# Handing attention's output to the expert layer: chunks opened early, late parts split from SBUF

## The chip, the cores and the metric

One core of a Trainium2 chip runs the kernel. The metric is device time in microseconds, the median of three runs. Engines: TensorE (PE in the profile; PEld is its weight load), VectorE (DVE), ScalarE (ACT), GpSimd (POOL) and SyncE (SP), which issues all of this kernel's DMAs.

## The reference

```python
# attention: B, H, S, D = 4, 8, 576, 64
scores = where(causal, -1e9, q @ k.T / sqrt(D));  local = softmax(scores) @ v
q_p = where(q > 0, q, exp(q) - 1) + 1
mem_out = (q_p @ M_prev) / (q_p @ z_prev + 1e-6)
attn = g * mem_out + (1 - g) * local              # g = sigmoid(beta), one per head
# expert layer: x is attn as 2304 tokens x 512, d_ff = 2048
h = x @ w_in;  y = (h * sigmoid(1.702 * h)) @ w_out
```

## The kernel before

Attention works on 16 pairs of heads, p = 0 to 15: batch b = p // 4 and part c = p % 4 of the 512 model columns. Each pair's output, transposed, is `xf`, 128 columns of x by 576 tokens in SBUF (one buffer). The expert layer works on eight chunks of tokens: chunk 0 is the first 256 tokens of batch 0 and is made by a short separate prologue (`first_queries`); chunk 1 is the other 320 tokens of batch 0; chunks 2 and 3, 4 and 5, 6 and 7 are the halves (288 tokens) of batches 1, 2 and 3. A chunk needs all four parts c of its batch.

Expert input must be more exact than one pass of TensorE's 32-bit rounded format, so each x is split into a high part `xh` (a ScalarE copy with rounding) and the rest `xl` (a GpSimd subtraction). Both tiles have two buffers, so chunk n takes the buffers of chunk n - 2. A block is 128 of the 2048 hidden columns: 12 matmuls, for each part c `xh` times both halves of the weight and `xl` times the high one, gathered in one of two PSUM banks `pm`. `gate` (line 698) copies the result to `hk`, on VectorE and ScalarE in turn (line 703), and stores it to the DRAM tensor `gd`. After attention, w_out is converted and the second matmul (`acc`) runs over all tokens.

The program is written out in slots. `at(slot, prio, fn)` (line 81) books a step of attention in a slot; `step` (line 735) runs the steps of one slot and then lets the generator `first_moe` (line 708) emit expert matmuls as filler until an estimate of TensorE time is used up: PACE (line 41) gives 2.2 us per slot up to slot 59 and 2.7 from 60 on, and `mm` (line 86) counts columns / 2.4 + 13 ns for each matmul of attention and filler. A pair takes eight slots (seven in batch 0). What is emitted is then reordered on each engine when the program is built, with the order of emission as priority; at run time each engine, SP too, takes its queue in order.

How x comes to the expert layer: `xstore` (line 654), two slots after a pair's last matmuls (slots 13, 20, 27, 34 for batch 0, then 43, 51, 59, 67 and so on to 131), stores `xf` to the DRAM tensor `xd[b]` (line 655), and after the fourth pair notes `xready[b]`. When the generator comes to a chunk that is not planned, it yields until its batch is ready, and calls `plan_x` (line 688): one load of all four parts in the next slot (line 692), `split_x` (line 207) in the slot after it, first matmul in the third. Together with chunks 2, 4 and 6 the next chunk is planned too, one slot later.

Of the kernel before, what the change touches and what calls it, by code (L numbers as in the profile page):

```python
# [9 lines left out]
F32R = mybir.dt.float32r  # L10
# [5 lines left out]
B, H, S, D = 4, 8, 576, 64  # L16
NP = H // 2
# [4 lines left out]
NK = DM // 128  # L22
# [7 lines left out]
def f32(ap):  # L30
    return ap.bitcast(F32)
# [3 lines left out]
def tile_attention_memory_moe(ctx, tc, kq, vq, mem, zz, beta, w_in, w_out, out):  # L35
    nc = tc.nc
    CH = 288
    NCH = S // CH
    MB = 1
# [7 lines left out]
    def pool(stack, name, bufs=1, **kw):  # L47
        return stack.enter_context(tc.tile_pool(name=name, bufs=bufs, **kw))
# [4 lines left out]
    mop = pool(left, "mop", 2, side="left")  # L53
# [14 lines left out]
    xd = [dr.tile([128, NK, S], F32, name=f"xd{b}") for b in range(B)]  # L68
# [4 lines left out]
    state = {"slot": -8, "pe": 0.0, "seq": 0, "sum": 0, "bank": 0}  # L73
# [7 lines left out]
    def at(slot, prio, fn):  # L81
        assert slot > state["slot"], (slot, state["slot"])
        state["seq"] += 1
        events.setdefault(slot, []).append((prio, state["seq"], fn))

    def mm(out, l, r, start, stop):
        n = out.free_size()
        state["pe"] += (n / 2.4 + 13) / 1000
        if l.dtype == F32:
            state["pe"] += 3 * n / 2400  # L90
        nc.tensor.matmul(out, l, r, start=start, stop=stop)  # L91
# [5 lines left out]
    def copy(eng, dst, src, scale=None):  # L97
        if eng == "A":
            kw = {} if scale is None else {"scale": scale}
            nc.scalar.activation(out=dst, in_=src, func=AF.Copy, **kw)  # L100
        elif eng == "V":
            if scale is None:
                nc.vector.tensor_copy(dst, src)
            else:
                nc.vector.tensor_scalar(out=dst, in0=src, scalar1=scale, scalar2=None, op0=ALU.mult)
        else:
            nc.gpsimd.tensor_copy(dst, src)

    def tt(eng, dst, a, b, op):
        (nc.vector if eng == "V" else nc.gpsimd).tensor_tensor(out=dst, in0=a, in1=b, op=op)  # L110

    def sub(eng, dst, src, hi):
        tt(eng, dst, src, f32(hi), ALU.subtract)
# [82 lines left out]
    chunks = [(b, 0, 256) for b in range(MB)] + [(b, 256, 320) for b in range(MB)]  # L196
    chunks += [(b, CH * ch, CH) for b in range(MB, B) for ch in range(NCH)]
    XW = max(n for _, _, n in chunks)
    xq = {}
    xplan = {}  # L200

    def new_x(n):
        xl = mop.tile([128, NK, XW], F32R, name="xl")
        xq[n] = [None, xl]
        return xl

    def split_x(n):
        w, xl = chunks[n][2], xq[n][1]
        xh = xq[n][0] = mop.tile([128, NK, XW], F32R, name="xh")
        for c in range(NK):  # L210
            copy("A", xh[:, c, :w], f32(xl[:, c, :w]))
            sub("P", xl[:, c, :w], f32(xl[:, c, :w]), xh[:, c, :w])

    def first_queries(b):
        K, fsm = [], []
# [119 lines left out]
    pairs = [(b, c) for b in range(B) for c in range(NP)]  # L335
    raws = {}
    prep = {}
    xready = {}

    K0 = [STEP * p for p in range(MB * NP)]  # L340
    K0 += [(K0[-1] + 8 if K0 else 0) + 8 * p for p in range(len(pairs) - len(K0))]
# [168 lines left out]
    def plan_attend(p):  # L510
        b, c = pairs[p]
        k0 = K0[p]
        P = prep[p]
        U = {}
        rest = b < MB
        qo = 256 if rest else 0
# [135 lines left out]
            tt("V", P["xf"][r, q0:q0 + n], po[r, :n], xb[r, :n], ALU.add)  # L652

        def xstore():
            nc.sync.dma_start(xd[b][:, c, qo:], P["xf"][:, qo:])
            del prep[p]
            raws.pop(p)
            if c == NP - 1:
                xready[b] = state["slot"]

        at(k0, 10, s_tail)
        at(k0 + 1, 10, max_tail)
# [15 lines left out]
        for u, (h, j) in enumerate(order):  # L678
# [4 lines left out]
            if j < 0 or j == 3:  # L683
                at(k + 1, 32, lambda h=h, ch=int(j > 0): xsum(h, ch))
        at(k + 2, 60, xstore)


    def plan_x(n, slot):
        b, a, w = chunks[n]

        def load():
            nc.sync.dma_start(f32(new_x(n)[:, :, :w]), xd[b][:, :, a:a + w])

        at(slot + 1, 5, load)
        at(slot + 2, 45, lambda: split_x(n))
        return slot + 3

    def gate(ps, n, blk):
        b, a0, w = chunks[n]
        t0 = b * S + a0  # L700
        def keep():
            h = mop.tile([128, XW], F32, name="hk", bufs=3)
            copy("AV"[blk % 2 == 0], h[:, :w], ps[:, :w])
            nc.sync.dma_start(gd[blk][:, t0:t0 + w], h[:, :w])

        at(state["slot"] + 1, 28, keep)

    def first_moe():
        after = 0
        for n, (b, _, w) in enumerate(chunks):  # L710
            if n not in xplan:
                while b not in xready:
                    yield 1
                xplan[n] = plan_x(n, state["slot"])
                if n >= 2 * MB:
                    xplan[n + 1] = plan_x(n + 1, state["slot"] + 1)
            for blk in range(NB):
                while blk not in wb or n not in xplan or state["slot"] < xplan[n]:
                    yield 1
                after += len(moe_ps) > 1  # L720
                pp, nm = moe_ps[int(after > LATE)]
                ps = pp.tile([128, 512], F32, name=nm)
                wi = wb[blk]
                k = 0
                for c in range(NK):
                    for s, mv in ((0, 0), (1, 0), (0, 1)):
                        mm(ps[:, :w], wi[:, s, 128 * c:128 * c + 128], xq[n][mv][:, c, :w], k == 0, k == 3 * NK - 1)
                        k += 1
                    yield 0
                gate(ps, n, blk)  # L730
                yield 0
# [42 lines left out]
    for blk in range(W0, NB):  # L774
        at(CONV[blk - W0], 58, lambda blk=blk: conv_in(blk))
    fill["gen"] = first_moe()
    while state["slot"] < K0[-1] + 16:
        step()
# [134 lines left out]
```

## Time and profile before

| | us |
|---|---|
| median of three runs | 684.53 |
| lowest, highest | 683.67, 687.51 |
| the profiled execution | 687.52 |
| its span | 685.6 |

The page of the profile gives each engine's busy share of the span. The chain of work is the profile's walk back from the last instruction: at each step to what released it, or to the instruction before it on its engine. Tables by window give each engine's busy time in a stretch, the granted clock of TensorE as a share of full speed, and the DMA engines' busy share.

### The profile page before, as it was taken

Reading aid. Unit: us, or ns where it says so; the run is one execution under the profiler, and the core shown is the slowest. Engines: PE = TensorE matmul, PEld = TensorE weight load, DVE = VectorE, ACT = ScalarE, POOL = GpSimd, SP = SyncE. Lnnn points to the kernel's source line nnn. Section 1 sums busy time; section 2 is a strip of 40 time slices with the busy share of each in tenths; the row PEclk is TensorE's granted clock in tenths of the full one; section 3 lists DMA queues with packets and bytes.
Section 4 is the critical chain, followed back from the end, with each engine's and each line's share of the span. In section 5 each row is a group of like instructions: output and inputs, shape, how many; then the busy total and the mean of one; then the engine's idle time right before and its main releaser. Section 6 shows DMA issues by size and latency. Waiting matters only on the chain.

```text
span 685.6 us, 12438 instructions
## 1 busy us (share of the span) xinstructions
PE 629.7 (92%) x3984; PEld 572.3 (83%) x3984; DVE 435.1 (63%) x1112; ACT 396.4 (58%) x960; POOL 263.7 (38%) x303
## 2 busy tenths in 40 slices
PE   4578898799987799999899997999999999999997
PEld 3468686689986699999899997999888888888897
DVE  4987765776758776677657634816865555555453
ACT  5676546787757775777576533614555445454453
POOL 3647545976636793566475202502400000000000
PEclk8699999999999999999999999999999999999999
DMA  8859758888557765766772128936444335344231
GB/s 252 270 158 262 217 139 239 231 211 222 150 156 206 206 186 168 216 164 181 236 206 71 44 79 292 323 115 222 152 123 142 109 102 154 94 126 133 68 125 55
DMA packets 71425, 116.70 MB, mean 170 GB/s; under 512 B 8768, under 2 KB 41024, under 8 KB 71360
## 3 DMA queue, kind: packets, MB, share of 16 engines
q1 hardware_dynamic: 71360, 115.91, 57.8%
q8 instruction: 32, 0.52, 0.3%
q14 instruction: 33, 0.27, 0.1%
HBM read 63.97 MB, written 27.79 MB: 134 GB/s over the span
## 4 chain that ended last, share of the span: by engine, by line
PE 73%; DMA 10%; DVE 7%; ACT 5%; issue 3%; SPq 1%; POOL 1%; ACTq 0%; DVEq 0%; POOLq 0%
PE acc L91 29%; PE pm L91 24%; PE po L91 9%; PE pt L95 6%; PE ps L91 5%; DMA gd<-hk 2%; DMA qr<-in_vq_dram 2%; DMA xl<-xd 2%; DMA xd<-xf 1%; DVE ps L499 1%; DMA fq<-in_vq_dram 1%; DVE ws L180 1%; DVE wr L182 1%; DVE ws L179 1%; DMA mr<-in_mem_dram 1%
## 5 line engine op out<-in xcount | busy, mean ns | idle before, releaser
L91 PE MATMUL pm<-xh,wi 128*128 128x288 f32 (+2 forms) x1024 | 221.3, 305 | 12.3 <-ACT hk L100 6.0
L91 PEld LDWEIGHTS pm<-xh,wi 128*128 128x128 f32 x1024 | 168.0, 192 | 15.9 <-ACT hk L100 6.9
L91 PE MATMUL acc<-gh,wo 128*128 128x512 f32 (+1 forms) x640 | 179.2, 368 | 0.0
L91 PE MATMUL pm<-xl,wi 128*128 128x288 f32 (+2 forms) x512 | 153.6, 301 | 0.1
L91 PEld LDWEIGHTS acc<-gh,wo 128*128 128x128 f32 x640 | 115.1, 189 | 20.1
L91 PE MATMUL acc<-gl,wo 128*128 128x512 f32 (+1 forms) x320 | 115.1, 368 | 0.0
L91 PEld LDWEIGHTS pm<-xl,wi 128*128 128x128 f32 x512 | 98.1, 192 | 0.7 <-POOL xl L110 0.3
L508 POOL TENSOR_SCALAR a<-a,sm,g 128x512 f32<-128x512 f32 (+3 forms) x112 | 71.9, 654 | 64.3 <-DVE sm L547 37.1
L499 DVE CUSTOM_DVE_ANT_0 ps<-ps,mask 128x256 f32<-128x256 f32 (+4 forms) x144 | 69.3, 495 | 20.7 <-PE ps L91 15.5
L813 DVE SCALAR_TENSOR_TENSOR gt<-gt,graw 128x512 f32<-128x512 f32 (+1 forms) x80 | 52.3, 654 | 45.5 <-ACT gt L812 45.0
L91 PE MATMUL po<-e,vs 128*128 128x320 f32 (+3 forms) x416 | 76.3, 308 | 4.5 <-ACT e L100 3.7
L505 ACT ACTIVATE a<-ps,nm 128x512 f32<-128x512 f32 (+3 forms) x112 | 60.2, 540 | 31.9 <-DVE nm L499 26.8
L812 ACT ACTIVATE gt<-graw 128x512 f32<-128x512 f32 (+1 forms) x80 | 47.0, 589 | 54.6 <-DVE gl L110 54.6
L110 DVE TENSOR_TENSOR gl<-gt,gh 128x512 fp32r<-128x512 f32 (+1 forms) x80 | 53.2, 665 | 37.2 <-ACT gh L100 34.1
L110 DVE TENSOR_TENSOR e<-pt,e 128x320 fp32r<-128x320 f32 (+1 forms) x120 | 56.4, 486 | 30.9 <-ACT e L100 30.3
L100 ACT ACTIVATE e<-pt 128x320 fp32r<-128x320 f32 (+4 forms) x136 | 55.7, 435 | 28.0 <-PE pt L95 15.0
L91 PEld LDWEIGHTS po<-e,vs 128*128 128x128 f32 x416 | 64.1, 192 | 9.2 <-ACT e L100 4.3
L100 ACT ACTIVATE gh<-gt 128x512 fp32r<-128x512 f32 (+1 forms) x80 | 47.0, 588 | 42.2 <-PE acc L91 39.6
L91 PEld LDWEIGHTS acc<-gl,wo 128*128 128x128 f32 x320 | 59.4, 189 | 9.9
L91 PE MATMUL ps<-W 128*128 128x512 f32 (+3 forms) x224 | 58.6, 347 | 4.6 <-DVE e L110 2.8
L95 PE MATMUL pt<-ident,a 128*128 128x128 f32 x296 | 57.5, 276 | 0.4 <-ACT a L505 0.4
L100 ACT ACTIVATE hk<-pm 128x288 f32<-128x288 f32 (+2 forms) x64 | 26.2, 409 | 52.5 <-PE pm L91 40.4
(132 smaller groups left out, 962.9 us busy)
## 6 DMA issues: line engine op xcount, KB each, us to landing
graw<-gd SPq DMA_DIRECT2D x64, 256.0 KB, 2.7
gd<-hk SPq DMA_DIRECT2D x96, 144.0 KB, 2.5
wraw<-in_w_in_dram SPq DMA_DIRECT2D x16, 512.0 KB, 4.3
wraw<-in_w_out_dram SPq DMA_DIRECT2D x16, 512.0 KB, 4.6
kqr<-in_kq_dram SPq DMA_DIRECT2D x12, 608.0 KB, 5.3
W<-hi SPq DMA_DIRECT2D x24, 272.0 KB, 3.6
W<-loq SPq DMA_DIRECT2D x48, 128.0 KB, 3.7
W<-lok SPq DMA_DIRECT2D x32, 144.0 KB, 3.3
```

Source lines behind the costliest of these rows:

```text
L91: nc.tensor.matmul(out, l, r, start=start, stop=stop)
L95: nc.tensor.transpose(out, in_, idn)
L100: nc.scalar.activation(out=dst, in_=src, func=AF.Copy, **kw)
L110: (nc.vector if eng == "V" else nc.gpsimd).tensor_tensor(out=dst, in0=a, in1=b, op=op)
L179: nc.vector.tensor_scalar(out=si, in0=si, scalar1=3, scalar2=None, op0=ALU.logical_shift_left)
L180: nc.vector.scalar_tensor_tensor(out=si, in0=raw[:, :, 1], scalar=-2 ** 31, in1=si, op0=ALU.bitwise_and, op1=ALU.bitwise_or)
L182: nc.vector.scalar_tensor_tensor(out=box["r"].bitcast(I32), in0=raw[:, :, 0], scalar=29, in1=si, op0=ALU.logical_shift_right, op1=ALU.bitw ...
L499: nc.vector.tensor_tensor_reduce(out=ps, in0=ps, in1=mk, op0=ALU.add, op1=ALU.min, scale=-0.125, scalar=1e38 if j == 0 else nm[:, j - 1:j] ...
L505: nc.scalar.activation(out=a, in_=ps, func=AF.Exp, scale=-1.0, bias=nm, accum_out=sm)
L508: (nc.vector if eng == "V" else nc.gpsimd).tensor_scalar(out=a, in0=a, scalar1=r, scalar2=gcol, op0=ALU.mult, op1=ALU.mult)
L812: nc.scalar.activation(out=t[:, :n], in_=raw[:, :n], func=AF.Tanh, scale=0.851)
L813: nc.vector.scalar_tensor_tensor(out=t[:, :n], in0=t[:, :n], scalar=1.0, in1=raw[:, :n], op0=ALU.add, op1=ALU.mult)
```

## The change

`plan_x` and `xready` go. A chunk is opened (`open_x`) when the generator comes to it, whether or not its batch is complete; with chunks 2, 4 and 6 the next one is opened too. Opening takes the buffers of `xl` and `xh`; each part that was stored by then is loaded by a DMA of its own, in the same slot, and split two slots later. A pair whose chunks are open when its `xstore` comes is no longer stored: `xf` is split straight into the chunks' `xh` and `xl`, and the first matmul may be emitted in the next slot after the fourth part.

```diff
-    def split_x(n):
-        w, xl = chunks[n][2], xq[n][1]
-        xh = xq[n][0] = mop.tile([128, NK, XW], F32R, name="xh")
-        for c in range(NK):
-            copy("A", xh[:, c, :w], f32(xl[:, c, :w]))
-            sub("P", xl[:, c, :w], f32(xl[:, c, :w]), xh[:, c, :w])
+    stored = {b: [] for b in range(B)}
+    left_x = {}
+
+    def split_x(n, c, src):
+        w = chunks[n][2]
+        xh, xl = xq[n]
+        copy("A", xh[:, c, :w], src)
+        sub("P", xl[:, c, :w], src, xh[:, c, :w])
+        left_x[n].discard(c)
+        if not left_x[n]:
+            xplan[n] = state["slot"] + 1
+
+    def open_x(n):
+        b, a, w = chunks[n]
+        xl = new_x(n)
+        xq[n][0] = mop.tile([128, NK, XW], F32R, name="xh")
+        left_x[n] = set(range(NP))
+        for c in stored[b]:
+            nc.sync.dma_start(f32(xl[:, c, :w]), xd[b][:, c, a:a + w])
+            at(state["slot"] + 2, 45, lambda c=c: split_x(n, c, f32(xl[:, c, :w])))
...
         def xstore():
-            nc.sync.dma_start(xd[b][:, c, qo:], P["xf"][:, qo:])
+            mine = [n for n, ch in enumerate(chunks) if ch[0] == b and (ch[1] or not rest)]
+            if any(n in left_x for n in mine):
+                for n in mine:
+                    split_x(n, c, P["xf"][:, chunks[n][1]:chunks[n][1] + chunks[n][2]])
+            else:
+                stored[b].append(c)
+                nc.sync.dma_start(xd[b][:, c, qo:], P["xf"][:, qo:])
             del prep[p]
             raws.pop(p)
-            if c == NP - 1:
-                xready[b] = state["slot"]
...
-    def plan_x(n, slot):
-        b, a, w = chunks[n]
-
-        def load():
-            nc.sync.dma_start(f32(new_x(n)[:, :, :w]), xd[b][:, :, a:a + w])
-
-        at(slot + 1, 5, load)
-        at(slot + 2, 45, lambda: split_x(n))
-        return slot + 3
...
-            if n not in xplan:
-                while b not in xready:
-                    yield 1
-                xplan[n] = plan_x(n, state["slot"])
+            if n >= MB and n not in left_x:
+                open_x(n)
                 if n >= 2 * MB:
-                    xplan[n + 1] = plan_x(n + 1, state["slot"] + 1)
+                    open_x(n + 1)
```

## Rows read from the trace of the kernel before

**Rows 1.** The page, part 1: busy us (share) x instructions of each engine.

```profile
PE 629.7 (92%) x3984; PEld 572.3 (83%) x3984; DVE 435.1 (63%) x1112; ACT 396.4 (58%) x960; POOL 263.7 (38%) x303
```

**Rows 2.** The chain of work over the span: start us, us, what.

```profile
...
228.93 4.46 DMA xd<-xf
233.40 4.48 DMA xl<-xd
...
416.05 7.23 DMA xl<-xd
...
435.25 49.32 PE pm L91 x372
484.57 197.13 PE acc L91 x960
```

**Rows 3.** Table by window: stretch, length, busy us (instructions), granted clock, DMA share, GB/s.

```profile
131.00:145.00 14.00, 9.62 (x55) 8.09 (x55) 8.04 (x33) 10.28 (x29) 11.03 (x13) 0.88 0.92 253
145.00:188.00 43.00, 43.00 (x320) 42.44 (x318) 32.85 (x104) 31.87 (x88) 29.04 (x33) 1.00 0.69 188
...
210.80:228.90 18.10, 13.62 (x93) 11.19 (x92) 15.29 (x51) 14.30 (x42) 11.69 (x14) 1.00 0.75 201
229.60:238.40 8.80, 6.08 (x46) 5.31 (x44) 6.46 (x18) 4.83 (x15) 4.24 (x5) 1.00 0.74 212
...
336.00:346.00 10.00, 7.77 (x50) 7.52 (x49) 5.99 (x24) 6.37 (x19) 7.70 (x10) 0.83 0.56 166
...
420.00:435.00 15.00, 11.08 (x69) 10.38 (x67) 12.31 (x19) 9.96 (x21) 7.29 (x7) 0.89 0.96 334
```

**Rows 4.** Timelines of ScalarE, VectorE and TensorE: start us, us [idle before, releaser].

```profile
130.61 0.43 ACT L100 ACTIVATE xf<-po 64x320 f32<-64x320 f32 x1 [0.37 <-PE po L91]
145.07 0.83 PE L91 MATMUL pm<-xh,wi 128*128 128x320 f32 x4
204.08 0.31 PE L91 MATMUL pm<-xl,wi 128*128 128x320 f32 x1
233.48 0.48 DVE L110 TENSOR_TENSOR xf<-po,xb 64x320 f32<-64x320 f32 x1 [2.10 <-DMA xd<-xf]
238.40 0.79 PE L91 MATMUL pm<-xh,wi 128*128 128x288 f32 x4 [1.27 <-ACT xh L100]
```

**Rows 5.** Timeline of SP's queue: start us, us of the issue, line, transfer.

```profile
132.87 0.38 SPq L655 DMA_DIRECT2D xd<-xf  x1
...
332.40 1.47 SPq L692 DMA_DIRECT2D xl<-xd  x1
...
343.00 0.57 SPq L692 DMA_DIRECT2D xl<-xd  x1
...
353.48 0.54 SPq L655 DMA_DIRECT2D xd<-xf  x1
```

**Rows 6.** Groups by shape: count, busy us, mean ns, idle before.

```profile
L110 POOL TENSOR_TENSOR xl<-xl,xh 128x288 fp32r<-128x288 f32 x24 | 18.6, 809 | 36.3 <-ACT xh L100 36.3
...
L100 ACT ACTIVATE xh<-xl 128x288 fp32r<-128x288 f32 x24 | 8.7, 435 | 5.9 <-DMA xl<-xd 5.8
```

**Rows 7.** Waits (us, times, longest): 334 to 346, 420 to 436; SP's, whole span.

```profile
PE pm L91 <- ACT hk L100: 2.2, 1, 2.2
...
ACT xh L100 <- DMA xl<-xd: 3.0, 1, 3.0
...
ACT ws L172 <- DMA wraw<-in_w_out_dram: 2.2, 1, 2.2
...
SPq L692 <- PE pm L91: 3.7, 2, 2.4
```

**Rows 8.** DMA issues over the span: transfer, count, KB each, median us to landing.

```profile
gd<-hk SPq DMA_DIRECT2D x96, 144.0 KB, 2.5
...
W<-loq SPq DMA_DIRECT2D x48, 128.0 KB, 3.7
...
xl<-xd SPq DMA_DIRECT2D x6, 576.0 KB, 5.2
```

More of the change, by code (lines that the diff above doesn't have):

```diff
@@ L337, in tile_attention_memory_moe @@
     prep = {}
-    xready = {}
     K0 = [STEP * p for p in range(MB * NP)]
```

## The prediction

> **What bounds the kernel now.** I read the page's first part, the chain, the windows, then the queues at the places the chain names. The page says TensorE is busy 92% of a 685.6 us span [rows 1]. That figure flatters: matmuls overlap, so I take free TensorE time from the weight loads (83% busy) as window length less PEld busy. Where the granted clock of a window is below 1.00, part of it ran at 1.2 GHz instead of 2.4, and I add the length times the missing share.
>
> The chain's order of time [rows 2] shows what sets the end: from 435.25 us on, nothing but TensorE (49.32 us of expert input, then 197.13 us of expert output). Ahead of that, the chain runs through x: the store of pair 7 at 228.93 takes 4.46 us, the load behind it 4.48 us, and at 416.05 a load takes 7.23 us. From 145 to 188, PEld is busy 42.44 of 43 us [rows 3]: TensorE is the bound there, as it is at the end. So a microsecond of expert work moved into a free place earlier is a microsecond off the end, as long as attention does not itself become the bound.
>
> Free places: the first matmul of chunk 1 starts at 145.07, its last at 204.08, the first of chunk 2 not before its split allows, at 238.40 [rows 4]. Ahead of each, attention runs alone with much of TensorE free (6.9 us in 210.8 to 228.9 [rows 3]). Two smaller holes lie at 336 to 346 and 420 to 435.
>
> The slots in the code are only priorities: chunk 5's load, emitted in slot 110, stands at 343.00, ahead of pair 12's store of slot 107, at 353.48 [rows 5]. Each engine's queue is reordered when the program is built; what counts is when data and buffers are there.
>
> **Which parts go direct.** By the code's own costs, eight slots of attention take 11.05 us, so PACE leaves 6.55 us of filler per eight slots up to slot 59 and 10.55 later. Chunk 1 is 16 blocks of 12 x (320/2.4 + 13) ns = 28.1 us. Before: pair 3 stores in slot 34, first block in slot 37, last in 67. After: chunk 1 is opened in slot 13 (reached there already), part 0 is loaded (its store has just been issued), parts 1 to 3 come direct, and the first block may follow in slot 35. Three periods give 19.7 us, the last 8.4 us some six slots: chunk 2 is reached in slot 65, two ahead of pair 7's xstore in slot 67. So chunks 2 and 3 load parts 0 to 2 and take part 3 direct. Their 51 us last some 39 slots from 68: chunk 4 is reached in slot 107, after pair 11 (99); chunk 6 in 139, after pair 15 (131). These get no direct part, only four small loads in place of a large one.
>
> **The change part by part.**
>
> (a) Chunk 1. Now: pair 3's store at 132.87, the load behind it, first matmul at 145.07 [rows 4, 5]. After: xf is complete at 131.04 [rows 4], well before SP came to its store; one ScalarE copy of 0.43 us and one GpSimd subtraction of 0.81 us [rows 6] make part 3 ready at 132.3, or by 134 where GpSimd's queue holds it. The free time in 131 to 145 is 14 - 8.09 = 5.9 us, plus 0.12 x 14 = 1.7 us of clock [rows 3]. Upper bound: 7.6, and with two blocks' parts 0 to 2 (there are two pm banks; 18 x 0.146 = 2.6 us) begun earlier, some 8 of what can follow through. Lower bound: 0, if batch 1's attention does not move up when TensorE is relieved. I take 5, nearer the top, as 145 to 188 has no free TensorE time.
>
> (b) Chunk 2. The same step at 228.93: first matmul at 230 to 231 in place of 238.40 [rows 2, 4]. Free there: 8.8 - 5.31 = 3.5 us [rows 3]. The first two blocks' parts 0 to 2 can go into the 6.9 us free before it: 18 x 0.133 = 2.4 us. Bounds 2 and 6; I take 4.5.
>
> (c) Chunk 4. ScalarE stands still for 3.0 us on the load that went out at 332.40; the hk copy is queued behind, both pm banks fill, TensorE idles 2.2 us [rows 5, 7] and comes back at 1.2 GHz for a part (granted 0.83 over this window [rows 3]). In all 2.5 + 1.7 = 4.2 us. After: parts 0 to 2 were stored long ago and can be loaded as soon as chunk 2's buffer is free; only a quarter of the bytes follows the last store. Bounds 0 and 4.2; I take 2.5.
>
> (d) Chunk 6. The same at 416.05, but here ScalarE also waits 2.2 us for w_out [rows 7], with the DMA engines 96% busy [rows 3]. Hole: 4.6 + 1.65 = 6.3 us. The w_out waits stay. Bounds -1 (more requests in a full queue) and 6; I take 2.
>
> (e) DMA. Gone: four stores (3 x 160 KB, 288 KB) and as many bytes of load, 1.5 MB; at the 253 GB/s of 131 to 145, 6 us of transfer where DMA is 92% busy [rows 3]. Issues on SP: 16 stores and 7 loads become 12 and 23, so 12 more at 0.38 to 0.57 us [rows 5], 5 to 7 us of SP in bursts of six and eight at chunks 2, 4 and 6. Behind them stand attention's W copies and the gd stores. I set both at nothing together: the bursts are hidden where parts were stored long before; without that cover, each costs up to 8 x 0.57 - 2 x 0.57 = 3.4 us.
>
> A 576 KB load lands in 5.2 us, a 144 KB gd store in 2.5 and 128 KB W copies, four of them in a row, in 3.7 each [rows 8]: less than two in turn would take, so small requests overlap. The Trainium skill speaks against the split loads: "DMA: Bandwidth & Descriptors", section "Bandwidth", asks for batches of 1 MiB and more, and its section "Anatomy of one DMA" (the GpSimd path) fits a fixed 2 us per DMA beside bytes over 436 GB/s. By that, an estimate from the page, one 576 KB load takes 3.4 us (the row has 5.2) and a 144 KB one 2.3 (the row agrees with 2.5), so four in a row 9.4; six us more at chunks 4 and 6, with (c) and (d) lost, would make 671 + 12 + 4.5 = 687.5 us, near the slower rival below. As the rows overlap, I don't take it.
>
> (f) ScalarE and GpSimd. The splits stay 28 and 28, only earlier. At pair 7 two copies (0.87 us) and two subtractions (1.62 us) stand in front of the next pair's work; GpSimd is busy 11.69 of 18.1 us there [rows 3], so hidden, or 1.6 us once. xf has one buffer; its next writer waited 2.10 us for the store [rows 4], and now waits for the subtraction instead. Nothing, or a small gain; I count nothing.
>
> Sum: 5 + 4.5 + 2.5 + 2 = 14 us. The profiled execution took 687.52 us around its 685.6 us span, 3 us above the median; I take the difference to the median, 684.53 - 14 = 670.5, say **671**. All low ends give 1 us, all high ones 24; for this case alone 664 to 679.
>
> **The rivals.**
> 1. Attention's own chain sets batch 1's end, so (a) is lost: 4.5 + 2.5 + 2 = 9, **675.5 us**. For it: a pair alone took 18.1 us from store to store (210.80 to 228.93) with TensorE free by a third. Against: 145 to 188 is full.
> 2. Filler is only shifted: (a) nothing, (b) its low 2, (c) and (d) nothing, as the reordered queues put the last part's copy where the load stood: **682.5 us**, no difference.
> 3. Slower: the loads at chunks 4 and 6 arrive later than the one large load. SP issues eight, four of which hold for the matmuls of the chunk before (L692 waited on TensorE for 3.7 us in all, twice [rows 7]); they go through one after another at 2.5 us each, 10 in place of 5.2; ScalarE's queue stands on the last part, hk copies and TensorE behind it. Each place: 4.8 + 2.4 and 1 us of clock = 8.2, so 684.5 - 9.5 + 16.4 = **691 us**. It decides from about 6.5 us at each place. Against it: parts 0 to 2 need no recent store.
> 4. The change doesn't do what it says: chunk 2 is reached after pair 7 and loads all four parts, (b) is lost: 5 + 2.5 + 2, **675 us**. Two slots stand between.
>
> **How the numbers follow.** Forecast 0.62, rival 1 0.13, rival 2 0.13, rival 3 0.08, rival 4 0.04. A measurement of this kernel tells some 0.5% (3.4 us) from no change. Faster: 0.62 + 0.13 + 0.04 = 0.79; same 0.13; slower 0.08. The range 663 to 683 takes in the forecast's own and rivals 1, 2 and 4, less the outer tails.
>
> **What would show it.** (a) first matmul of chunk 1 at 131 to 135, and pair 7's part up to 5 us earlier. (b) no store for pair 7, and TensorE on chunk 2 within 3 us of xf. (c), (d) no 3 us wait of ScalarE on xl at chunk 4, and a shorter one at chunk 6. (e) 12 stores and 23 loads. I am wrong if the chunk starts move up and pair 7's end doesn't, or if SP's bursts hold up W copies.

## The result and the profile after

| | before | after |
|---|---|---|
| median of four runs, us | 684.10 | 692.34 |
| lowest, highest | 682.67, 687.51 | 690.91, 693.09 |
| the profiled execution (its span) | 687.52 (685.6) | 693.09 (691.3) |

After / before is 1.0111, with a 95% interval of 1.0069 to 1.0153: slower by some 8 us, where 13 us faster was forecast. Of both kernels the slowest of the four runs is the profiled one, so the spans differ by 5.7 us and the medians by 8.2.

The page of after, part 1, as [rows 1]: busy us (share) x instructions.

```profile
PE 633.6 (92%) x3984; PEld 575.3 (83%) x3984; DVE 432.3 (63%) x1112; ACT 397.8 (58%) x960; POOL 265.4 (38%) x303
```

No engine has noticeably more work than before. So the time was lost in waiting, and the chain says for what. After's chain over the span, as [rows 2]: start us, us, what.

```profile
172.14 5.46 DMA xl<-xd
...
198.59 5.96 DMA xl<-xd
...
288.88 5.13 DMA xl<-xd
...
340.80 4.83 DMA xl<-xd
...
419.99 2.95 DMA xd<-xf
...
439.90 26.98 PE pm L91 x191
...
469.70 20.81 PE pm L91 x156
490.51 197.14 PE acc L91 x960
```

The last stage is as long as before (197.14 and 197.13 us) and begins at 490.51 in place of 484.57; all of the loss lies ahead of it. The loads of x stand on the chain at four places spread over the span; in [rows 2] two were read, both behind the last store of a batch.

The change was built as the slot count of the prediction said. After's DMA issues, as [rows 8] (transfer, count, KB each, median us to landing), show 12 stores and 23 loads; of pairs 1, 2, 3 and 7 no store is left.

```profile
gd<-hk SPq DMA_DIRECT2D x96, 144.0 KB, 2.4
W<-loq SPq DMA_DIRECT2D x48, 128.0 KB, 3.5
xd<-xf SPq DMA_DIRECT2D x11, 288.0 KB, 2.8
xl<-xd SPq DMA_DIRECT2D x22, 144.0 KB, 4.5
...
xd<-xf SPq DMA_DIRECT2D x1, 160.0 KB, 3.1
xl<-xd SPq DMA_DIRECT2D x1, 160.0 KB, 2.8
```

A load of 144 KB lands after 4.5 us (median), a 576 KB load of before after 5.2 [rows 8]. A quarter of the bytes saves 0.7 us.

Waits over the whole span (total us, times, longest), before:

```profile
ACT xh L100 <- DMA xl<-xd: 6.0, 4, 3.0
```

And after:

```profile
ACT xh L100 <- DMA xl<-xd: 22.4, 10, 4.5
```

ScalarE stood 22.4 us on loads of x, ten times, where it stood 6.0 us, four times. SP's queue in after (start us, us of the issue, line, transfer) shows why there are so many:

```profile
165.72 0.41 SPq L676 DMA_DIRECT2D xd<-xf  x1
...
172.14 0.42 SPq L227 DMA_DIRECT2D xl<-xd  x1
...
281.98 0.54 SPq L676 DMA_DIRECT2D xd<-xf  x1
...
288.88 0.57 SPq L227 DMA_DIRECT2D xl<-xd  x1
...
289.98 0.42 SPq L227 DMA_DIRECT2D xl<-xd  x1
```

The store of pair 4 goes out at 165.72 and the load of that part for chunk 2 6.4 us behind it; behind pair 9's store at 281.98 come the first two loads for chunk 4, at 288.88 and 289.98, when chunk 2's buffers have just come free. By the prediction's count opening emitted these loads in slots 65 and 107, but once each part has its own load, each can be moved forward in the reordered queue until it stands behind its own store or the release of its buffer, and its xh copy with it. ScalarE's timeline in after (start us, us [idle before, releaser]):

```profile
136.57 1.22 ACT L100 ACTIVATE hi<-kqr 128x1216 fp32r<-128x1216 f32 x1 [2.15 <-DMA qr<-in_vq_dram]
137.70 0.45 ACT L100 ACTIVATE xh<-xf 128x320 fp32r<-128x320 f32 x1
...
177.62 0.44 ACT L100 ACTIVATE xh<-xl 128x288 fp32r<-128x288 f32 x1 [3.29 <-DMA xl<-xd]
177.97 0.85 ACT L100 ACTIVATE e<-pt 128x384 fp32r<-128x384 f32 x2
...
294.03 0.44 ACT L100 ACTIVATE xh<-xl 128x288 fp32r<-128x288 f32 x1 [3.80 <-DMA xl<-xd]
294.38 0.48 ACT L100 ACTIVATE e<-pt 128x384 fp32r<-128x384 f32 x1
```

Behind each waiting copy stands attention's own work, the softmax copy `e`, up to 3.29 and 3.80 us late. (Such waits alone don't show a loss: e1 below has 13.0 us of them and loses nothing.) Before, one load of all four parts could not go ahead of the batch's last store, so its split never stood in front of the attention that makes the batch.

Windows of after, as [rows 3], and some more (stretch, length, busy us of PE, PEld, DVE, ACT, POOL with instructions, granted clock, DMA share, GB/s):

```profile
131.00:145.00 14.00, 10.19 (x50) 8.45 (x48) 7.55 (x28) 9.52 (x25) 12.30 (x14) 0.76 0.82 212
145.00:188.00 43.00, 42.12 (x305) 41.12 (x306) 29.15 (x96) 27.85 (x77) 21.77 (x26) 1.00 0.58 165
...
420.00:435.00 15.00, 13.26 (x97) 12.55 (x96) 8.48 (x15) 6.69 (x14) 3.83 (x3) 1.00 0.84 298
```

```profile
197.00:217.00 20.00, 14.72 (x85) 12.69 (x83) 11.56 (x39) 11.71 (x33) 10.71 (x11) 0.83 0.59 164
285.00:320.00 35.00, 33.78 (x257) 32.71 (x255) 22.85 (x68) 20.27 (x57) 17.15 (x20) 1.00 0.73 200
320.00:335.00 15.00, 13.30 (x100) 13.02 (x101) 11.56 (x40) 13.03 (x37) 10.83 (x12) 1.00 0.51 137
335.00:352.00 17.00, 14.12 (x96) 13.56 (x95) 9.80 (x31) 9.61 (x29) 8.21 (x10) 0.90 0.69 201
445.00:484.00 39.00, 37.88 (x288) 37.64 (x287) 16.66 (x31) 10.24 (x23) 8.08 (x6) 1.00 0.56 183
```

The same five of before:

```profile
197.00:217.00 20.00, 17.12 (x114) 14.58 (x115) 15.88 (x54) 13.86 (x40) 13.41 (x14) 1.00 0.59 158
...
285.00:320.00 35.00, 35.00 (x275) 34.80 (x274) 26.47 (x88) 24.61 (x70) 18.55 (x22) 1.00 0.68 190
320.00:335.00 15.00, 15.00 (x116) 14.79 (x115) 10.07 (x31) 11.03 (x30) 8.59 (x10) 1.00 0.81 221
335.00:352.00 17.00, 14.77 (x102) 14.30 (x101) 10.12 (x34) 13.18 (x39) 13.50 (x16) 0.90 0.72 194
445.00:484.00 39.00, 39.00 (x298) 39.00 (x297) 18.25 (x34) 12.05 (x26) 6.81 (x6) 1.00 0.55 179
```

With free time as length less PEld, as in the prediction, the same view gives for the whole stretch from 97 to 484:

| us | 97–197 | 197–217 | 217–260 | 260–285 | 285–335 | 335–400 | 400–484 |
|---|---|---|---|---|---|---|---|
| before | 17.0 | 5.4 | 10.6 | 0.2 | 0.4 | 3.0 | 4.9 |
| after | 15.6 | 7.3 | 6.9 | 0.3 | 4.3 | 3.9 | 7.3 |

The holes that the change aimed at did become smaller (97 to 197 by 1.4 us, 217 to 260 by 3.7). But 1.9 us came back at 197 to 217, where chunk 1, begun earlier, was used up earlier and the clock now fell to 0.83 (part of the window at 1.2 GHz), 3.9 at 285 to 335, which had been full, and 3.3 from 335 on. The sum grows by 3.9 of the 5.9 us by which the last stage begins later. The table leaves out the clock, since work at the lower clock takes longer but counts as busy: 131 to 145 was granted 0.76 against 0.88 [rows 3], 197 to 217 0.83 against 1.00. By the prediction's own rule (length times the missing share), summed over windows of 8 us from 97 to 484, the clock took 10.2 us in after and 6.7 in before. Free time and clock together grow by 7.4 us, more than the 5.9.

### The profile page after: what moved, and what is told of

Read it like the earlier page. It is cut to its first block, busy times and chain, and to the rows that moved or that the text cites. A ratio compares the mean times of both kernels' runs of the same rounds, so it can differ in the third digit from the quotient of the medians.

```text
span 691.3 us, 12443 instructions
## 1 busy us (share of the span) xinstructions
PE 633.6 (92%) x3984; PEld 575.3 (83%) x3984; DVE 432.3 (63%) x1112; ACT 397.8 (58%) x960; POOL 265.4 (38%) x303
## 4 chain that ended last, share of the span: by engine, by line
PE 67%; DMA 13%; ACT 7%; DVE 5%; SPq 4%; issue 3%; POOL 1%; ACTq 0%; DVEq 0%; POOLq 0%
PE acc L91 29%; PE pm L91 21%; PE po L91 7%; PE ps L91 5%; PE pt L95 5%; DMA xl<-xd 3%; DMA kqr<-in_kq_dram 3%; DMA gd<-hk 2%; DMA xd<-xf 1%; ACT a L520 1%; DMA qr<-in_vq_dram 1%; SPq L419 1%; ACT e L100 1%; DMA wraw<-in_w_in_dram 1%; DMA vr<-in_vq_dram 1%
## 5 line engine op out<-in xcount | busy, mean ns | idle before, releaser
L110 DVE TENSOR_TENSOR gl<-gt,gh 128x512 fp32r<-128x512 f32 (+1 forms) x80 | 53.3, 666 | 37.2 <-ACT gh L100 34.0
L91 PE MATMUL ps<-W 128*128 128x512 f32 (+3 forms) x224 | 60.6, 356 | 5.3 <-DVE e L110 2.6
```

## The experiments

Each kernel was run in five rounds beside the kernel before; ratios are to that, with a 95% interval. The kernel before itself gave single times between 678.7 and 688.8 us, so only ratios are compared, and a mechanism seen in one trace counts as an indication where no ratio stands behind it. "The changed kernel" (ratio 1.0111) is the reference for the experiments that start from it.

### The change in parts: e1, e2, e3

The chunks in a set are opened as in the changed kernel; the others are planned as before (complete batch, one load).

```diff
-            if n >= MB and n not in left_x:
+            if n in NEW and n not in left_x:         # e1: (1,)  e2: (1, 2, 3)  e3: (4, 5, 6, 7)
                 open_x(n)
...
+            elif n >= MB and n not in NEW and n not in xplan:
+                while len(stored[b]) < NP:
+                    yield 1
+                open_old(n, state["slot"])
...
```

> Only chunk 1 is opened early (part 0 loaded, parts 1 to 3 direct); chunks 2 to 7 come by store and one load, as before. Theory W (ScalarE's in-order queue stands on loads of parts that were stored a moment before, so the early and split loads cost): there is one such load here, at 98, where TensorE waited 1.3 us, so nothing is lost and the 2.3 us of early matmuls at 97 to 131 are kept: 680 to 684 us against 684. Rival C (opening chunk 1 early is itself the loss, as pair 4's store was already 4.5 us late in the changed kernel): 687 to 690 us.

Measured: 684.93 beside 684.23, ratio 1.0012 (0.9985 to 1.0039). Chunk 1 alone is worth nothing. SP's queue in this kernel, the stores of pairs 4 and 7:

```profile
167.36 0.39 SPq L693 DMA_DIRECT2D xd<-xf  x1
...
231.85 0.54 SPq L693 DMA_DIRECT2D xd<-xf  x1
```

Pair 4 is stored at 167.36 (before 161.27) and pair 7 at 231.85 (before 228.93 [rows 2]): 6 and 3 us later. Of both, 2 us were there from pair 0 on (96.81 and 94.83), so attention lost 4 us up to the first pair of the batch and 1 us up to its last. It did not move up. Chunk 2 needs that last pair, so it could begin no earlier, while chunk 1 ended 7 us earlier (last matmul at 197.01, before 204.08 [rows 4]).

The early matmuls did fill free places: from 97 to 484 free TensorE time is 38.3 us, before 41.5. But the clock, by the rule above, took 11.8 us where it took 6.7. The stretch behind chunk 1 in e1, and ScalarE's waits on loads of x over its span:

```profile
197.00:217.00 20.00, 15.05 (x92) 13.81 (x91) 13.34 (x46) 13.52 (x39) 10.75 (x12) 0.83 0.53 148
```

```profile
ACT xh L100 <- DMA xl<-xd: 13.0, 6, 4.8
```

> Chunks 1 to 3 as in the changed kernel, chunks 4 to 7 as before. Theory W: the waits of ScalarE at 174 to 177 and around 200 to 206 stay (some 6 us of free TensorE time), the earlier start of chunk 2 (6 us) stays too, the waits at 290 to 408 go: 683 to 687 us. Rival C: 690 us or more, little better than the changed kernel's 692.

Measured: 691.95, ratio 1.0110 (1.0075 to 1.0144): the whole loss, with chunks 4 to 7 as before. The step from e1 to e2 is chunks 2 and 3: three small loads each and one direct part. Windows of e2:

```profile
285.00:335.00 50.00, 50.00 (x389) 49.51 (x388) 36.33 (x116) 35.28 (x98) 26.38 (x29) 1.00 0.71 194
335.00:352.00 17.00, 11.82 (x71) 11.59 (x71) 8.56 (x31) 11.44 (x33) 14.20 (x18) 0.80 0.58 177
```

TensorE is full from 285 to 335, where after lost most, and then waits 5.18 us for chunk 4's split, until 340.68. The whole loss thus comes without the hole at 285 to 335.

> Chunks 1 to 3 as before, chunks 4 to 7 opened as in the changed kernel: four loads of 144 KB each in place of one of 576 KB, nothing direct. Theory W: ScalarE waits some 3 to 4 us on each of three or four loads, TensorE loses 2 us at each: 688 to 692 us against 684. Rival C: 683 to 685 us, no loss.

Measured: 686.93, ratio 1.0040 (1.0010 to 1.0069). Nothing is direct here; four small loads in place of one cost 2.7 us. ScalarE's waits on loads of x are 15.5 us in six (6.0 in four before), and 285 to 335 is no longer full (PEld 45.40 of 50 us). The two parts do not add up: 1.0110 and 1.0040 alone, 1.0111 together.

### Whose queue the splits stand in: e4, e5

e4: the changed kernel, with the xh copies of direct parts on VectorE. e5: the changed kernel, with those of loaded parts on GpSimd, so that ScalarE waits for no load of x.

```diff
-        copy("A", xh[:, c, :w], src)
+        copy(eng, xh[:, c, :w], src)     # e4: "V" if src is xf, else "A";  e5: "P" if src is xl, else "A"
```

> The changed kernel, but the high parts of direct parts are copied by VectorE and not by ScalarE. Theory L (the gain at chunk 1 was lost because pair 3's copy stands in ScalarE's queue behind the hi copy, which waits for a load until 136.6): chunk 1 begins about 3 us earlier, 688 to 690 us against the changed kernel's 692. If ScalarE's place in the order doesn't matter there: 691 to 693.

Measured: 691.26, ratio 1.0105 (1.0070 to 1.0141), no better than the changed kernel. In ScalarE's queue the direct copy of pair 3 stood behind `hi` until 137.70 (above); it is free of that here, and 131 to 145 has more work in it (PEld 10.89 us at full clock, in after 8.45 at 0.76), but the total stays. So the late direct copy was not the cause.

> The changed kernel, but the high parts of loaded parts are copied by GpSimd (which does their subtraction anyway), so ScalarE's queue never stands on a load of x. Theory W (ScalarE's waits for the split loads are the loss): 685 to 689 us against the changed kernel's 692. Theory P (chunks 2 and 3's matmuls, emitted two slots earlier, take TensorE from attention and run out earlier at the next chunk): 691 to 693 us.

Measured: 687.99, ratio 1.0058 (1.0024 to 1.0091). ScalarE waits for no load of x here, and the point estimate lies 0.5% below the changed kernel's. The intervals overlap, so it is not shown that half of the loss hangs on these waits; and e1 (13.0 us of them, no loss) and e2 (12.6 us, the whole loss) say that their total does not set the time.

### One load, and a later place: e6, e7, e8

e6: one load for all parts that are stored when a chunk is opened. e7: the first matmul of chunks 2 and 3 may be emitted in the third slot after the last part instead of the first (slot 70, as before, instead of 68). e8: both.

```diff
-        for c in stored[b]:
-            nc.sync.dma_start(f32(xl[:, c, :w]), xd[b][:, c, a:a + w])
+        k = len(stored[b])
+        nc.sync.dma_start(f32(xl[:, :k, :w]), xd[b][:, :k, a:a + w])
...
-            xplan[n] = state["slot"] + 1
+            xplan[n] = state["slot"] + (3 if n in (2, 3) else 1)
```

> The changed kernel, but the parts that are stored when a chunk is opened come by one load each chunk (parts 0 to 2 for chunks 2 and 3, all four for chunks 4 to 7), so nothing is loaded and split behind each single pair. Theory W: three early waits at chunks 2 and 3 become one, those at 4 to 7 are as before the change: 685 to 688 us. Theory P: 690 to 693 us.

Measured: 690.24, ratio 1.0080 (1.0052 to 1.0108). Windows of e6:

```profile
285.00:320.00 35.00, 35.00 (x275) 34.80 (x275) 27.09 (x88) 24.75 (x69) 18.30 (x20) 1.00 0.70 197
320.00:335.00 15.00, 15.00 (x116) 14.77 (x116) 10.16 (x30) 10.47 (x29) 8.08 (x9) 1.00 0.79 190
335.00:352.00 17.00, 13.09 (x84) 12.85 (x83) 9.18 (x33) 12.78 (x37) 13.66 (x18) 0.80 0.61 187
445.00:484.00 39.00, 37.55 (x286) 37.31 (x285) 14.85 (x28) 11.04 (x24) 7.61 (x7) 1.00 0.52 168
```

From 285 to 335 TensorE is full again, as before. With e2, which is full there, and e3, which is not, this puts the 3.9 us lost there on the split loads of chunks 4 to 7. The losses at 335 to 352 (with a lower clock) and 445 to 484 stay.

> The changed kernel, but the first matmul of chunk 2 may be emitted in slot 70, as before the change, not in 68. Theory P: attention has its old priority over chunks 2 and 3, 684 to 688 us. Theory W: the loads and copies are as in the changed kernel, 691 to 693 us.

Measured: 690.94, ratio 1.0092 (1.0057 to 1.0127). Alone, the later place gives little. e6 came out in theory P's range and e7 beside theory W's, so each theory failed with its own cure alone.

> One load for the stored parts, and the first matmul of chunk 2 in slot 70. Theory W: as with one load alone, 685 to 688 us. Theory P: as with slot 70 alone, 684 to 688 us. If both cost: below either alone, 680 to 685.

Measured: 685.23, ratio 0.9991 (0.9969 to 1.0014). Together, the two take the loss away, which neither did alone (0.3% and 0.2%), but nothing is gained: chunk 1 early, four pairs without store and load, and the time of before. Behind chunk 1 its trace has the hole of e1 again:

```profile
197.00:217.00 20.00, 14.66 (x86) 13.03 (x86) 14.64 (x48) 15.10 (x43) 11.57 (x13) 0.83 0.52 134
```

From 97 to 484 free time is 38.3 us, 3.2 less than before, and the clock took 10.2 us, 3.5 more.

### The place alone, without the change: f1, g1, g2, g3, and g4

The kernel before, chunk 2 only. f1: load and splits one slot earlier, the first matmul two (slot 68). g1: load and splits one slot earlier, the matmul in slot 70. g2 and g3: load and splits as before, first matmul in slots 72 and 74. g4: e8 with slot 72.

```diff
+        if n == 2:                               # f1 and g1
+            load()
+            at(slot + 1, 45, lambda: split_x(n))
+            return slot + 1                      # g1: slot + 3
         at(slot + 1, 5, load)
         at(slot + 2, 45, lambda: split_x(n))
-        return slot + 3
+        return slot + (5 if n == 2 else 3)       # g2; g3: 7
```

> The kernel before, with one thing changed: chunk 2's load, split and first matmul are emitted in slots 67 and 68, two slots earlier, as in the changed kernel; data come by store and load as before. Theory P (the earlier place in the order alone costs, by giving chunks 2 and 3 precedence over attention): 686 to 689 us against 684. If the place matters only together with the changed kernel's data: 683 to 685 us.

> The kernel before; chunk 2's load is emitted in slot 67 and its splits in slot 68, one earlier each, while its first matmul stays at slot 70. If the loss of 0.78% of f1_before_slot68 comes from its matmuls' place ahead of attention's: no loss here, 684, ratio 0.998 to 1.002. If it comes from the place of the load and the splits in SP's, ScalarE's and GpSimd's queues: 687 to 688, ratio 1.006 to 1.008.

> The kernel before; chunk 2's first matmul is emitted in slot 72 in place of 70, all else stays. If a place two slots earlier costs because expert work comes ahead of attention's: the same or faster here, 682 to 684, with pair 9 stored before 279.6 us and chunk 3 begun after 287.8. If any other order of the queues costs something (the order of the kernel before is merely a lucky one): slower by 0.3 to 0.8%, 686 to 690.

> The kernel before; chunk 2's first matmul is emitted in slot 74, four later than before. Precedence of expert work: attention again earlier, pair 9 stored by 278 us, but free TensorE time after pair 7 grows by up to 3 us; together 682 to 686. A lucky order: slower by 0.3 to 0.8%, with no order between slots 68, 72 and 74.

> The changed kernel with one load for the stored parts, first matmul of chunks 2 and 3 in slot 72 (e6_one_load has 68: 1.008; e8_both 70: 0.9991). Precedence: 0.995 to 1.000, no worse than e8_both. A lucky order: slower than e8_both by 0.3 to 0.8%, ratio 1.002 to 1.007.

Measured, with the issue of pair 15's store as the mark of attention's end (SP's queue in each kernel's trace):

| kernel | first matmul of chunk 2 | pair 15's store at | ratio (interval) |
|---|---|---|---|
| f1 | 68 | 414.48 | 1.0078 (1.0049–1.0107) |
| before | 70 | 412.47 | 1 |
| g1 | 70, load and splits early | 410.80 | 1.0028 (1.0005–1.0051) |
| g2 | 72 | 410.04 | 1.0035 (1.0009–1.0061) |
| g3 | 74 | 408.41 | 1.0081 (1.0055–1.0107) |
| e6 | 68, opened early, one load | 414.33 | 1.0080 |
| e8 | 70, same | 412.25 | 0.9991 |
| g4 | 72, same | 408.45 | 0.9996 (0.9969–1.0024) |
| changed kernel | 68, split loads | 419.99 | 1.0111 |

Neither theory of the expectations holds throughout: g2 and g3 came out as a lucky order says, g4 as precedence says, g1 between its two ranges. Attention's end does move in one direction, by 1.6 to 3.8 us per two slots, with and without the change: the earlier expert work is emitted, the later attention ends. (One trace each; g1, with no matmul moved, shifts it by 1.7 us too.) But the time does not follow attention's end: in the kernel before it is least at slot 70 and 0.35 to 0.8% longer on both sides. With chunks opened early and one load, slots 70 and 72 take the same time and only 68 costs. In f1, windows and a timeline show the price of the early side, the run-out at chunk 4:

```profile
335.00:352.00 17.00, 13.54 (x88) 13.30 (x87) 9.36 (x34) 13.32 (x39) 13.35 (x17) 0.80 0.62 184
445.00:484.00 39.00, 37.52 (x286) 37.29 (x285) 14.93 (x28) 10.75 (x24) 7.69 (x7) 1.00 0.51 170
```

```profile
341.47 1.33 PE L91 MATMUL pm<-xh,wi 128*128 128x288 f32 x4 [3.46 <-ACT xh L100]
```

PEld is busy 13.30 and 37.29 us in place of 14.30 and 39.00, at a lower granted clock in the first, and TensorE waits 3.46 us for chunk 4's splits. e6 (3.91 us) and e2 (5.18 us), which also have chunk 2 in slot 68, wait at the same place, with the same clock of 0.80. In g3 the free time lies elsewhere:

```profile
320.00:335.00 15.00, 13.00 (x102) 12.74 (x100) 11.08 (x35) 6.24 (x17) 5.46 (x6) 1.00 0.82 248
...
445.00:484.00 39.00, 37.75 (x285) 37.28 (x284) 18.08 (x33) 12.10 (x26) 6.33 (x5) 1.00 0.52 163
```

Whether slot 70 is best in the kernel before because it balances the two, or because the kernel before happens to have a good order there, these runs can't tell: g1, which moves no matmul, still costs 0.28%.

### Fewer waits and another pace: f2, f3, f4

f2: e8 with the loaded parts' xh on GpSimd (as e5). f3: e8 with a slower filler from slot 20 to 51 and a faster one from 52 on. f4: the kernel before with that pace.

```diff
-    PACE = ((20, 2.2), (60, 2.2), (9999, 2.7))
+    PACE = ((20, 2.2), (52, 2.0), (9999, 2.7))
```

> One load for the stored parts, first matmul of chunk 2 in slot 70, and the high parts of loaded parts copied by GpSimd, so that ScalarE never stands on a load of x (10.1 us in the run without this). Theory W: 681 to 684 us, faster than both kernels. If those waits are no longer on the path, or GpSimd's queue takes them over: 684 to 687 us.

Measured: 696.19, ratio 1.0152 (1.0115 to 1.0189), slower than everything else. Between 352 and 400, full in before, TensorE waits once 4.5 us for VectorE's copy `e`, and pair 15 is stored at 420.68. What helped with split loads (e5) costs with one load; why was not followed further.

> One load for the stored parts, slot 70, and PACE 2.0 us up to slot 51 and 2.7 from 52 on, so that chunk 1 comes later and attention of pairs 4 and 5 first. Theory A (the gain at chunk 1 is lost because its matmuls displace attention at 145 to 190 and run out before pair 7 ends): pairs 4 and 5 are stored 3 us earlier, pair 7 ends 2 to 4 us earlier, 680 to 683 us. If attention's own chain sets pair 7's end: 684 to 686 us.

Measured: 687.10, ratio 1.0055 (1.0038 to 1.0072), in neither range. Pairs 4 and 5 are stored at 163.39 and 188.68 (e8: 164.48 and 187.30), not 3 us earlier.

> The control: the kernel before with that PACE. Theory A: chunk 1 starts at 145 there and has less room, 682 to 686 us against 684.

Measured: 681.28 beside 683.36, ratio 0.9970 (0.9953 to 0.9987): below the range expected, and the only kernel here whose interval lies below the kernel before. Its pair 15 is stored at 406.19, its last stage begins at 477.42. From 97 to 484 both terms fall: free time is 37.2 us, and the clock took 5.0. With chunks opened early, the same pace costs 0.6% (f3 against e8).

## Why the prediction was wrong

**What bounds the kernel.** The failing step is the sentence "a microsecond of expert work moved into a free place earlier is a microsecond off the end, as long as attention does not itself become the bound". The condition was named and then not examined. That 145 to 188 is full [rows 3] shows that TensorE is the bound in that stretch, not that the work in it can be done in any order: attention and expert work share it, and chunk 1 moved ahead let no attention move up (e1). In e8 those 43 us are as full (PEld 42.53), and yet the hole behind them, 197 to 217, is larger: 7.0 us free (PEld 13.03 of 20) where before had 5.4. The prediction credited each closed hole with its clock and charged none for a hole that opens elsewhere. In e1 and e8 free time from 97 to 484 fell by 3.2 us each, and the clock took 5.1 and 3.5 us more, the largest part of it in 197 to 217 (0.83, before 1.00), behind a wait of TensorE of 2.44 and 2.43 us (before: 1.72). So by these traces what the early work filled was lost again, mostly at the hole that it left. This is read from one trace of each kernel; no run holds the clock fixed.

**(a) Chunk 1, 5 us: measured 0.** e1, 1.0012. Parts 0 to 2 of the first blocks did go early (97 to 131 lost 1.4 us of its free time), but the first full block began at 138.20 in after, not by 134, because the direct copy queued on ScalarE behind a copy that waited for a DMA. That mis-sized the step; it did not decide it, as e4 shows. Rival 1 named what did, that batch 1's attention doesn't end earlier, at 0.13; but its 675.5 us kept (b), (c) and (d). The prediction's own first sign of being wrong came true: chunk 1's start moved up, pair 7's end did not.

**(b) Chunk 2, 4.5 us.** No store of pair 7 is left, and the hole after it closed (217 to 260: 3.7 us less free time, near the 4.5). But the first matmul with part 3 came at 237.91 in place of 238.40, since pair 7's last xf ended at 235.11 rather than 228.42: what the direct path saved, attention had lost in the same batch. Chunk 3 then ran out earlier, and f1 shows that chunk 2's earlier place, without any direct part, costs 0.78% (of which its load and splits alone, moved one slot in g1, 0.28%). The step that failed is that a place gained by one stage is kept by the next.

**(c) Chunk 4, 2.5 us: no gain.** The range had zero as its lower end. e3 measures (c) and (d) together as a loss of 2.7 us (1.0010 to 1.0069). The hole stayed: in after TensorE waits 2.27 us for chunk 4's split, until 346.14, where it waited 2.2 [rows 7], and 335 to 352 is granted 0.90 as before. ScalarE waits 4.5 us once between 334 and 346, where it waited 3.0 [rows 7]. The step said that parts 0 to 2 "were stored long ago and can be loaded as soon as chunk 2's buffer is free". Where the queues are reordered, nothing holds such a load back until it is needed; it went out right behind the newest store or the release of the buffer, and the split stood waiting in front of attention's work at pair after pair; that opened the new hole at 285 to 335.

**(d) Chunk 6, 2 us.** Between 420 and 435 PEld is busy 12.55 us against 10.38 [rows 3], at full clock against 0.89. But attention ends 7.5 us later in after, and the hole only moved back with it. From 420 to 445, before and after:

```profile
420.00:445.00 25.00, 20.83 (x143) 20.12 (x142) 20.03 (x32) 15.48 (x32) 14.13 (x14) 0.93 0.97 335
420.00:445.00 25.00, 20.88 (x141) 19.93 (x140) 18.14 (x30) 14.51 (x29) 10.35 (x9) 0.93 0.92 320
```

The free time (4.9 and 5.1 us) and the clock are the same. ScalarE's waits on x there did become short (0.2 us), as the prediction said, but it waits 5.5 us for w_out in place of 2.2 [rows 7]. Besides, 400 to 420 and 445 to 484, full before, lost 2.2 us, and e3, which holds (c) and (d) alone, is a loss.

**(e) DMA and SP, nothing.** The counts were right, and W copies land as before (3.5 us, 3.7 in [rows 8]). But the rows that I took against the Trainium skill misled: the 144 KB gd stores (2.5 us [rows 8]) are no measure for a load of x of the same size, which took 4.5. The Trainium skill's rule speaks against split loads ("DMA: Bandwidth & Descriptors", section "Bandwidth"), and e3 against before, and e8 against e7, agree with its direction. The estimate from the Trainium skill's section "Anatomy of one DMA" (the GpSimd path), 2.3 us for such a load, is not what the trace shows (4.5). The price, as far as the traces show it, came through ScalarE's queue, not in the transfers: the DMA share from 285 to 335 was no higher than before (0.66 against 0.72, the two windows taken together).

**(f) Splits, nothing.** The number of copies is the same, 28. That each was put at nothing because its engine had room is, by the traces, the error behind (c): an engine that takes its queue in order has no room while its next instruction waits.

**The rivals.** Rival 3 had a part of the mechanism, ScalarE's queue standing on a part, and its time, 691, is near 692.34; but it put it at the last part of chunks 4 and 6, while the runs show it at pair after pair, and the larger part of the loss in chunks 2 and 3 (e1, e2). Rival 2 ("filler is only shifted", 682.5) comes nearest to e8 (685.23), where the losses are taken out. Rival 4 is refuted by the counts.

What stays open: why e6 and e7, each worth 0.2 to 0.3%, are worth 1.2% together, and why e2 and e3 don't add up. Both point to the order of the queues as a whole, as do f1 and g1 to g3; no single wait was shown to carry it. Open too is what the early work would be worth if the clock did not fall behind chunk 1.

## What to carry to other kernels

A full engine that serves two streams gained nothing here when one stream was moved ahead, since the other did not move up. Look for who waits on the stream that is pushed back (here the batch's last pair) before counting a filled hole as a gain, and charge the hole that opens where the early work runs out, with its clock. Where queues are reordered at build time, splitting one late load into parts lets every part's consumer move forward to stand, waiting, in front of other work on an in-order engine; keep one load (e8 against e7: 0.9991, 1.0092), or tie the consumers to the point of need (not tried here). Before crediting a change with the microseconds of its holes, move the same work by two places in the kernel before: here that alone was worth 0.3 to 0.8%, as much as the effect in question.

## What was not expected of the hardware

Loads of x of 144 KB landed after 4.5 us, of 576 KB after 5.2, and stores of 144 KB after 2.4 (all medians): by the medians the size of a load hardly counted here, and a store of the same size was no guide to it. Single loads of 144 and 160 KB ranged from 2.1 to 6.0 us.
